# A TensorE loop of nine guarded rounds, a new place for wo among the loads, wider q matmuls and one projection moved ahead, in a decode-attention kernel

## Chip, cores, metric

One core of one Trainium2 chip at a time. The metric is the device time of one execution in microseconds (us); lower is better. A traced execution also has a span, about 1.3 us shorter than its device time.

## The reference, cut to what matters

```python
# x: 1 x 448.  k_cache, v_cache: 8 heads x 65536 x 256, bf16.  16 query heads, two for each KV head.
g = sigmoid((x * gate_w).sum(-1))
a = softmax(((x @ wq) heads) @ k_cache^T / 16) @ v_cache  @ wo     # one query token
b = (relu(x @ W_gate) * (x @ W_up)) @ W_down
out = g * a + (1 - g) * b
```

K and V are 537 MB of the 549 MB that must be read once. One token's arithmetic is small beside that.

## The kernel before

K and V come as 32 + 32 tiles of 8.39 MB (128 partitions of 64 KB). SyncE issues all of these loads, in one order, into three ring slots. A load waits until its slot's last reader is done: the QK matmuls of a K tile, the PV matmuls of a V tile. VectorE transposes K tiles in place (8 instructions a tile) before QK.

The plan gives each operation an engine and a key (a planned time). An engine runs its operations in the order of the keys, so a key decides order alone.

```python
order = [("wq", 0, 8.7), ("k", 0, TILE), ("gu", 0, 7.7), ("wd", 0, 3.8)]
for n in range(1, NT):
    order.append(("k", n, TILE))
    if n >= NTH - 1:
        order.append(("v", n - (NTH - 1), TILE))
for i in range(NT - NTH + 1, NT - 1):          # V 29, V 30
    order.append(("v", i, TILE))
order.append(("wo", 0, 7.3))                   # wo of heads 0 to 4
# then V 31 in five pieces, then the rest of wo in four
...
ROUND = (0, 1, 2, 0, 1, 0, 2, 1)
slot, held, freed = {}, {2: ["gu", "dn"]}, {}  # slot 2 first holds W_gate, W_up, W_down
...
# W_down's projection ("dn"), reading slot 2
l_["dn"] = op("pe", max(tg + 12.2, tL["wd", 0]), f_dn, [l_["hT"], a3])
...
# QK of K tile n, in two halves
qk[n, b] = op("pe", tk + 9 * (b + 1), f_qk(n, b, sl), [tr[4 * b + 3], xcopy, aexp.get(n - 2), c_ps[n % 2]])
...
def emit_loop(self, its, eng, go):             # TensorE: one loop body, seven rounds
    with eng.Fori(0, len(its)):
        for o in its[0]:
            eng.wait_ge(go, 1).then_inc(go, -1)
            o.fn(eng).then_inc(self.esem["pe"], 1)
...
pl.emit("pe", pe[:cut[0]], nc.tensor)          # straight code up to QK of K tile 3
pl.emit_loop(its, nc.tensor, go)               # seven rounds
pl.emit("pe", pe[cut[-1]:], nc.tensor)         # straight code from QK of K tile 31
```

In the loop TensorE doesn't know which semaphore count a round needs; GpSimd waits in its place and gives it one "go" for each operation.

With these keys QK of K tile 0 precedes dn. K tile 2 goes into slot 2, so its load waits for dn.

## Time and profile before

| | before |
|---|---|
| device time, median of 3 | 1278.33 us (1277.96 to 1279.88) |
| the traced execution | 1280.09 us, span 1278.8 us |
| PE, VectorE (DVE) busy | 33%, 50% |
| DMA | 549 MB, 430 GB/s over the span |

The profile's table of slices (40 slices of 32 us; a digit is the busy share in tenths) says what bounds the kernel, and the table of DMA queues tells instruction fetches (q8 is TensorE's) from data:

```profile
PE   3624323334223431224331343321433323233245
...
DVE  2588633465433655434555444555434656335600
...
DMA  9999999999999999999999999999999999999998
...
q1 hardware_dynamic: 12930, 549.03, 99.6%
q8 instruction: 11, 0.18, 0.1%
```

DMA is full everywhere, so time can be gained only where the queue runs dry or works slowly. There is one such place early on. The timeline of before around QK of K tile 0 (start us, length us, engine, line, operation, count, and in brackets the idle time ahead of it with what ended it):

```profile
52.99 6.35 PE L371 MATMUL ST<-ring,xc 128*16 128x512 bf16 x64
...
59.16 1.51 PE L382 MATMUL A_ps<-ring,hT 128*1 128x224 bf16 x28
...
60.70 0.80 SPq L475 DMA_DIRECT2D ring<-in_A_k_cache_dram  x2
...
64.04 17.66 DVE L360 STREAM_TRANSPOSE ring<-ring 128x2048 uint32<-128x2048 uint32 x8 [3.96 <-DMA ring<-in_A_k_cache_dram]
...
84.86 4.50 DVE L360 STREAM_TRANSPOSE ring<-ring 128x2048 uint32<-128x2048 uint32 x2 [3.16 <-DMA ring<-in_A_k_cache_dram]
```

QK of tile 0 (L371), dn (L382), and only then, at 60.70 us, K tile 2's load. The transposes start as soon as a tile has landed: tile 1 at 64.04, tile 2 at 84.86 us, 20.82 us apart, where a tile takes 19.35. The waits of SyncE's queue name the culprit. In the windows of 2 us the last three columns are TensorE's granted clock, the DMA share and GB/s:

```profile
SPq L475 <- PE A_ps L382: 37.9, 1, 37.9
```

```profile
56.00:58.00 2.00, 2.00 (x24) 0.66 (x20) 0.00 (x0) 0.00 (x0) 0.00 (x0) 0.50 1.26 532
58.00:60.00 2.00, 2.00 (x38) 1.23 (x32) 0.61 (x1) 0.00 (x0) 0.00 (x0) 0.90 1.17 496
60.00:62.00 2.00, 0.67 (x14) 0.38 (x10) 0.08 (x1) 1.40 (x2) 0.00 (x0) 1.00 0.96 328
62.00:64.00 2.00, 0.00 (x0) 0.00 (x0) 0.00 (x0) 0.00 (x0) 0.00 (x0) 1.00 0.74 262
```

This view counts a packet with all its time and bytes where it starts, so a single window jumps (before's from 52 to 54 us has a share of 0.53 with 16 packets under way all along). The share of 0.74 from 62 to 64 us therefore doesn't show the hole by itself; the trace's packet records do. Of q1's packets 16 are under way at 60.5 us, 9 at 61.5, 11 at 62, 14 at 63 and 16 again at 64 us. A load is spread over the core's 16 DMA engines, and its semaphore is raised by each of them (16 records for every load of a tile). The trace's semaphore records therefore tell when the first and the last engine finished each load. I call the gap between them the lag.

### The profile page before, as it was taken

How to read it: one execution, taken by the hardware profiler on the slowest of the kernel's cores; microseconds unless marked ns; L12 is line 12 of the kernel's file. 1: busy time of each engine (PE TensorE's matmuls, PEld its weight loads, DVE VectorE, ACT ScalarE, POOL GpSimd, SP SyncE). 2: the span in 40 equal slices, each digit the busy share in tenths (PEclk: the TensorE clock that was granted, in tenths of full speed). 3: DMA queues.
4: the chain of work that ended last, by engine and by line, in shares of the span. 5: the costliest groups of instructions: out<-in, count | busy, mean ns of one | idle time of the engine just before them, and what ended most of it. 6: DMA issues, size and time to landing. Idle time of an engine off the chain costs nothing. (4 is left out here: it accounts for less than half of the span.)

```text
span 1278.8 us, 10158 instructions
## 1 busy us (share of the span) xinstructions
PE 427.7 (33%) x4600; PEld 169.4 (13%) x4600; DVE 633.1 (50%) x421; ACT 63.1 (5%) x124; POOL 4.1 (0%) x21
## 2 busy tenths in 40 slices
PE   3624323334223431224331343321433323233245
PEld 2401101111001110002110111110111101011111
DVE  2588633465433655434555444555434656335600
ACT  0000000000000100001000010000100001000000
POOL 1000000000000000000000000000000000000000
PEclk8555666656666565666656666656666656666567
DMA  9999999999999999999999999999999999999998
GB/s 396 427 427 437 439 429 433 429 445 428 428 433 439 433 433 430 433 441 430 433 433 433 437 433 430 433 435 437 433 433 430 441 433 428 433 435 435 433 413 346
DMA packets 12951, 549.27 MB, mean 430 GB/s; under 512 B 1283, under 2 KB 3590, under 8 KB 3974
## 3 DMA queue, kind: packets, MB, share of 16 engines
q1 hardware_dynamic: 12930, 549.03, 99.6%
q8 instruction: 11, 0.18, 0.1%
q14 instruction: 6, 0.05, 0.0%
q10 hardware_dynamic: 4, 0.00, 0.0%
HBM read 549.03 MB, written 0.00 MB: 429 GB/s over the span
## 5 line engine op out<-in xcount | busy, mean ns | idle before, releaser
L360 DVE STREAM_TRANSPOSE ring<-ring 128x2048 uint32<-128x2048 uint32 x256 | 565.4, 2275 | 399.0 <-DMA ring<-in_A_k_cache_dram 399.0
L371 PE MATMUL ST<-ring,xc 128*16 128x512 bf16 x2048 | 224.9, 614 | 745.8 <-PEq L86 687.6
L371 PEld LDWEIGHTS ST<-ring,xc 128*16 128x16 bf16 x2048 | 66.7, 121 | 889.6 <-issue 827.2
L402 PE MATMUL O<-ring,ptp 128*4 128x512 bf16 x2048 | 150.4, 457 | 34.1 <-DMA ring<-in_A_v_cache_dram 29.8
L486 ACT ACTIVATE P_sb<-ST,nmb 128x512 bf16<-128x512 f32 x32 | 45.1, 1411 | 1103.2 <-DVE nmb L484 1103.2
L484 DVE TENSOR_REDUCE nmb<-ST 128x1 f32<-128x512 f32 x32 | 22.1, 690 | 115.7 <-PE ST L371 115.7
L402 PEld LDWEIGHTS O<-ring,ptp 128*4 128x4 bf16 x2048 | 56.4, 99 | 127.9 <-issue 60.0
L412 DVE CAST o_sb<-O 128x512 bf16<-128x512 f32 x8 | 5.5, 692 | 80.3 <-PE O L402 80.3
L505 DVE TENSOR_TENSOR P_sb<-P_sb,hs 128x1024 bf16<-128x1024 bf16 x16 | 18.9, 1222 | 9.3 <-ACT hs L499 9.3
L510 PE MATMUL PT<-identb,P_sb 128*128 128x128 bf16 x128 | 16.2, 307 | 16.7 <-PEq L86 13.9
L452 PE MATMUL M_ps<-xT,ring 128*128 128x1 bf16 x84 | 9.5, 205 | 16.8 <-DMA ring<-in_B_W_up_dram 16.8
L510 PEld LDWEIGHTS PT<-identb,P_sb 128*128 128x128 bf16 x128 | 12.4, 139 | 19.1 <-issue 16.8
L519 ACT COPY ptp<-PT 128x256 bf16<-128x256 bf16 x32 | 10.3, 375 | 23.8 <-PE PT L510 23.8
L332 PE MATMUL M_ps<-ring,P_sb 128*128 128x256 bf16 x64 | 9.7, 329 | 2.9 <-DMA ring<-in_A_wq_dram 2.9
L452 PEld LDWEIGHTS M_ps<-xT,ring 128*128 128x128 bf16 x84 | 7.2, 152 | 17.4 <-issue 17.0
L486 ACT ACTIVATION_READ_ACCUMULATOR P_sb<-ST,nmb 128x1 f32 x32 | 8.4, 263 | 0.0
L332 PEld LDWEIGHTS M_ps<-ring,P_sb 128*128 128x128 bf16 x64 | 7.5, 119 | 4.9 <-issue 3.0
L455 PE MATMUL M_ps<-xT,ring 128*64 128x1 bf16 x56 | 7.8, 276 | 0.0
L435 DVE STREAM_TRANSPOSE scr<-P_sb 128x128 uint32<-128x128 uint32 x1 | 0.3, 313 | 12.8 <-ACT P_sb L434 12.8
L495 PE MATMUL M_ps<-identf,hs 128*2 128x128 f32 x8 | 2.5, 308 | 10.9 <-PEq L86 9.7
L382 PE MATMUL A_ps<-ring,attnT 128*1 128x224 bf16 x64 | 4.6, 305 | 2.7 <-DMA ring<-in_A_wo_dram 2.7
L455 PEld LDWEIGHTS M_ps<-xT,ring 128*64 128x64 bf16 x56 | 5.4, 191 | 0.4
(74 smaller groups left out, 61.5 us busy)
## 6 DMA issues: line engine op xcount, KB each, us to landing
ring<-in_A_v_cache_dram SPq DMA_DIRECT2D x1, 4096.0 KB, 30.0
ring<-in_A_wq_dram SPq DMA_DIRECT2D x1, 3072.0 KB, 10.2
ring<-in_A_wo_dram SPq DMA_DIRECT2D x1, 2240.0 KB, 32.4
ring<-in_A_v_cache_dram SPq DMA_DIRECT2D x1, 2048.0 KB, 24.6
ring<-in_B_W_down_dram SPq DMA_DIRECT2D x1, 1568.0 KB, 21.2
ring<-in_B_W_gate_dram SPq DMA_DIRECT2D x1, 1344.0 KB, 32.8
ring<-in_B_W_up_dram SPq DMA_DIRECT2D x1, 1344.0 KB, 35.5
ring<-in_A_v_cache_dram SPq DMA_DIRECT2D x1, 1024.0 KB, 26.6
```

The lines of the kernel that those rows point to most:

```text
L332: ins = e.matmul(QN_ps, xw3[:, k_, 31 - j:159 - j], rhs, start=(j == 0 and kt == 0), stop=(j == J - 1 and kt == R3))
L360: return lambda e: e.transpose(v, v)
L371: ins = e.matmul(bank[32 * w:32 * w + 16, :], xc[:, x0:x0 + 16], ktv[sl][:, u0:u0 + 16, c, :, r_], start=(b == 0 and c == 0 and r_ == 0), ...
L402: ins = e.matmul(OP[32 * g:32 * g + 4, :], ptp[:, col:col + 13:4], ring[sl][:, k * 512:(k + 1) * 512], start=(a == 0 and k < 4), stop=(a = ...
L412: o1 = op("dv", tn, lambda e: e.tensor_copy(o_sb[:], OP[:]), [pv[n], last.get(("otr", h - 1))])
L452: e.matmul(GU_ps[:, c:c + 1], wf3[which][:, kt * F + ft:(kt + 1) * F:FT], xT[:, kt:kt + 1], start=(kt == 0), stop=False, skip_group_check= ...
L455: ins = e.matmul(GU_ps[64 * half:64 * half + 64, c:c + 1], wfh[which][:, ft:F // 2:FT], xT[:, R3 + half:R3 + half + 1], start=False, stop= ...
L484: smax[n] = op("dv", tk + 22, lambda e, n=n, NM=NM, t_=t_: e.tensor_reduce(NM[:, t_:t_ + 1], ST[n % 2][:], AX.X, ALU.max, negate=True), [q ...
L486: aexp[n] = op("ac", tk + 23, lambda e, n=n, t_=t_, NM=NM, RS=RS: e.activation(P_sb[:, t_:2048:4], ST[n % 2][:], ACTF.Exp, bias=NM[:, t_:t ...
L505: rsc = op("dv", tt, lambda e, X=X, pb=pb: e.tensor_tensor(pb, pb, X[:, 12:16].unsqueeze(1).to_broadcast([128, 256, 4]), ALU.mult), [h7, a ...
L510: ins = e.transpose(PT[rd][:, s * 128:(s + 1) * 128], P_sb[:, (rd * 8 + s) * 128:(rd * 8 + s + 1) * 128], identb[:, :])
L519: ins = e.copy(dst, src)
```

## The change

The intent: take the first and last heads into TensorE's loop, so that its program is shorter. Rounds 0 and 8 are partial, so each part of the body stands under guards on the round number. Since code in the loop names its ring slot, a tile can be in it only if it has the slot that its place in the round has. V 29 therefore moves to slot 0, which K 31 frees late; wo is loaded ahead of it to fill that time. K 0, V 30 and V 31 don't fit and stay outside. On the side, q is computed with matmuls of 512 columns instead of 256, and dn moves ahead of QK of K tile 0. The diff, cut to its core:

```diff
+        with eng.Fori(0, n) as i:
+            ...
+            for lo, hi, rounds in parts:
+                with ExitStack() as st:
+                    if lo > 0:
+                        st.enter_context(eng.If_ne(i, lo - 1))
+                    if hi < n:
+                        st.enter_context(eng.If_lt(i, hi))
+                    body(rounds[0])
...
-        for i in range(NT - NTH + 1, NT - 1):
-            order.append(("v", i, TILE))
-        order.append(("wo", 0, 7.3))
+        order += [("wo", 0, 7.3), ("v", NT - 3, TILE), ("v", NT - 2, TILE)]
...
+        LASTS = (0, 1, 2, 0, 1, 0)
-                sl = r if m < 0 else ROUND[m % 8] if m < 8 * (H - 1) else m % 8 % 3
+                sl = r if m < 0 else ROUND[m % 8] if m < 8 * (H - 1) else LASTS[m - 8 * (H - 1)]
...
-            for j in range(J):                       # f_q: 16 x 4 matmuls of 256 columns
+            for h in range(H):                       # f_q: 8 x 4 matmuls of 512 columns
...
-                l_["dn"] = op("pe", max(tg + 12.2, tL["wd", 0]), f_dn, [l_["hT"], a3])
+                l_["dn"] = op("pe", tg + 12.2, f_dn, [l_["hT"], a3])
+                assert tg + 12.2 < tL["k", 0] + 20
...
-                    qk[n, b] = op("pe", tk + 9 * (b + 1), f_qk(n, b, sl), [...])
+                    qk[n, b] = op("pe", tk + (9 * (b + 1) if n else 20 + b), f_qk(n, b, sl), [...])
...
+        span = [(1, H + 1), (1, H), (1, H + 1), (0, H), (1, H), (0, H), (1, H)]   # rounds of the seven parts
-        pl.emit("pe", pe[:cut[0]], nc.tensor)
-        pl.emit_loop(its, nc.tensor, go)
-        pl.emit("pe", pe[cut[-1]:], nc.tensor)
+        pl.emit("pe", pe[:heads[0][0]], nc.tensor)
+        pl.emit_loop(H + 1, span, nc.tensor, go)
+        pl.emit("pe", pe[end:], nc.tensor)
```

## The prediction

> **What bounds the kernel now.** The DMA queue. In the table of slices DMA is at 9 in all but the last, while PE is busy 33% and DVE 50% of 1278.8 us. From K tile 3 (landed 104.19 us) to K tile 31 (1187.95 us) the trace's DMA landings are 56 tiles in 1083.76 us: 19.353 us for 8.39 MB, 433.5 GB/s. The Trainium skill, "DMA: Bandwidth & Descriptors", "Where 436 GB/s comes from", gives 435.2 GB/s as ceiling; the trace agrees to 0.4%. All bytes at the measured rate are 1267 us, so only the ends and single stalls can gain.
>
> **What the change does.**
>
> 1. Guards: the loop takes in heads 0 and 7, with more branches on TensorE's sequencer. TensorE waits 22 to 23 us before most QK groups (waits view), and a K tile is issued some 30 us before its own transfer starts (issue to landing 51.3 us), a V tile 17 us. Branches of some us per round are hidden: 0 us.
>
> 2. Fewer instruction fetches. The queue table shows 11 of 16 KB on q8. In the packet records each takes its DMA engine 1.07 us, and the next 64 KB packet there 2.9 instead of 2.42 us: 1.5 us lost on one of 16 engines. The Trainium skill, "Runtime: NRT & Kernel Launch", "Instruction fetch mechanics", says TensorE refills in 16 KiB blocks; the packets agree, and later rounds fetch nothing (none from 245 to 1180 us). I count 2100 instructions of program after, 2800 before: 8 fetches, estimated. It matters only on the engine that finishes last: it lags the first by 2.8 us from tile 2 on, and by 4.34 us after the fetch at 1251 us. Worth 0 to 1.5 us, by luck; I take 0.6.
>
> 3. The hidden part: W_down's projection (dn) now precedes QK of K tile 0. K tile 2's load waits for dn (waits view: 37.9 us, once) and is issued at 60.70 us, only 0.2 us before the first engine runs out of K tile 1. Tiles 1 and 2 land 20.82 us apart instead of 19.35: a hole of 1.47 us, kept to the end. After, dn should run at 53.6 to 55.1 us and the load be issued near 55.2. Gain 1.5 us.
>
> 4. q as 32 matmuls of 512 columns for 64 of 256: the group of 9.67 us shrinks by 1 us (estimated), but W_down and K tile 1 queue behind other loads anyway: 0 us.
>
> 5. wo heads ahead of V 29: same bytes. V 29 waits for K 31's QK (done at 1209.1 us before), and wo's 2.29 MB run out 6 us after V 28. The first engines may idle 1 us, the last, which decides, should not: 0 us.
>
> **Sum.** 1278.3 - 1.5 - 0.6, about 1276.3 us. Range 1274.5 to 1278.3. Faster by over 2%: 1%; within: 98%; slower: 1%.
>
> **What would show it.** K tile 2's load issued near 55 us; K 1 and K 2 landing 19.4 us apart; 19.35 us from tile to tile; 7 to 9 packets on q8; engines at most 4.4 us apart at the last landing; DVE busy unchanged; V 29 issued 2 to 4 us before wo's last packet.
>
> **What would make it wrong.** A fetch that stalls TensorE over 10 us at a skipped part, so that a slot comes free late; refetching in every round (dozens of q8 packets, up to 5 us); fetches on the last engine; V 29 issued after wo's packets end, 1 to 3 us.

## The result and the profile after

| | before | after |
|---|---|---|
| device time, median | 1278.42 us (4 runs, 1277.96 to 1279.88) | 1277.62 us (4 runs, 1277.48 to 1277.77) |
| traced execution, span | 1278.8 us | 1276.2 us |
| TensorE's instruction fetches (q8) | 11 | 8 |
| last landing of the last load (wo) | 1276.59 us | 1273.92 us |

The ratio is 0.9992, interval 0.9974 to 1.0009: the same within 2%, and by this interval not told from no change, though the highest run of after (1277.77) is under the lowest of before (1277.96). Five more rounds below gave 0.9989.

The same views of the kernel after. The slices and the queues first:

```profile
PE   3633322334223431224331343321333313233255
...
DVE  2698633465433655434555444555434655335600
...
DMA  9999999999999999999999999999999999999998
...
q1 hardware_dynamic: 12930, 549.03, 99.7%
q8 instruction: 8, 0.13, 0.0%
```

Then the timeline around QK of K tile 0, where L378 is QK, L389 dn:

```profile
53.73 2.40 PE L389 MATMUL A_ps<-ring,hT 128*1 128x224 bf16 x24 [0.53 <-DVE hT L468]
...
55.92 0.58 PE L389 MATMUL A_ps<-ring,hT 128*1 128x224 bf16 x4
56.13 4.43 PE L378 MATMUL ST<-ring,xc 128*16 128x512 bf16 x62
56.54 4.40 SPq L483 DMA_DIRECT2D ring<-in_A_k_cache_dram  x2
...
63.21 17.66 DVE L367 STREAM_TRANSPOSE ring<-ring 128x2048 uint32<-128x2048 uint32 x8 [1.89 <-DMA ring<-in_A_k_cache_dram]
...
83.50 4.50 DVE L367 STREAM_TRANSPOSE ring<-ring 128x2048 uint32<-128x2048 uint32 x2 [2.63 <-DMA ring<-in_A_k_cache_dram]
```

K tile 2's load is issued at 56.54 us, 5 us before the first engine has finished K tile 1 (61.53 us); in before that margin was 0.75 us (60.70 to 61.45), too little. (The prediction's 0.2 us is the same margin, counted to the end of the first engine's last packet.) SyncE's wait for dn is 3.7 us shorter, and in the packet records 16 packets or more are under way at each half microsecond from 60 to 64 us. The windows:

```profile
SPq L483 <- PE A_ps L389: 34.2, 1, 34.2
```

```profile
60.00:62.00 2.00, 0.56 (x8) 0.06 (x2) 0.69 (x1) 0.65 (x1) 0.00 (x0) 1.00 0.99 426
62.00:64.00 2.00, 0.00 (x0) 0.00 (x0) 0.79 (x1) 0.74 (x2) 0.00 (x0) 1.00 1.14 492
```

Tile 2 still follows tile 1 by 20.29 us at the *last* engine, though the first has its two tiles 19.34 us apart. The difference is lag, and it has to be read engine by engine. The next table is worked out from the DMA semaphore records of the two traces: when the first engine, the mean of the 16 and the last engine had finished a load.

| load landed, us: first / mean / last engine | before | after |
|---|---|---|
| K 1 | 61.45 / 62.21 / 64.02 | 61.53 / 62.05 / 63.18 |
| K 2 | 82.05 / 82.65 / 84.84 | 80.87 / 81.59 / 83.48 |
| K 31 | 1185.14 / 1186.46 / 1187.95 | 1183.86 / 1185.06 / 1186.89 |
| V 28 | 1204.50 / 1205.81 / 1207.30 | 1203.23 / 1204.42 / 1206.25 |
| last wo load | 1272.49 / 1273.93 / 1276.59 | 1272.08 / 1272.77 / 1273.92 |

At K 2 the first engine has gained 1.2 us, and it keeps that through 58 tiles to V 28: nothing is won or lost in between. At the end the last engine has gained 2.67 us, 1.62 us more than at V 28. In before, the fetch at 1251 us fell on the engine that was then last and widened the lag from 2.79 to 4.34 us; in after, none did. But this before-trace is of a run of 1280.09 us, well over its median: a pair of traces isn't the difference of two medians.

### The profile page after: what moved, and what is told of

Its sections match the earlier page's. It is cut to its first block, busy times and chain, and to the rows that moved or that the text cites. A ratio compares the mean times of both kernels' runs of the same rounds, so it can differ in the third digit from the quotient of the medians.

```text
span 1276.2 us, 10216 instructions
## 1 busy us (share of the span) xinstructions
PE 426.9 (33%) x4568; PEld 167.3 (13%) x4568; DVE 633.4 (50%) x421; ACT 63.3 (5%) x124; POOL 4.1 (0%) x21
## 5 line engine op out<-in xcount | busy, mean ns | idle before, releaser
L378 PE MATMUL ST<-ring,xc 128*16 128x512 bf16 x2048 | 223.9, 611 | 745.6 <-PEq L86 745.6
L378 PEld LDWEIGHTS ST<-ring,xc 128*16 128x16 bf16 x2048 | 68.3, 120 | 887.0 <-issue 886.1
L341 PE MATMUL QN<-ring,P_sb 128*128 128x512 bf16 x32 | 8.9, 448 | 3.1 <-DMA ring<-in_A_wq_dram 3.1
L389 PE MATMUL A_ps<-ring,attnT 128*1 128x224 bf16 x64 | 4.6, 306 | 0.7 <-DMA ring<-in_A_wo_dram 0.6
```

The lines of the kernel that those rows point to most:

```text
L341: ins = e.matmul(QN_ps, xw3[:, k_, 31 - h:159 - h], rhs, start=(h == 0 and kt == 0), stop=(h == H - 1 and kt == R3))
L378: ins = e.matmul(bank[32 * w:32 * w + 16, :], xc[:, x0:x0 + 16], ktv[sl][:, u0:u0 + 16, c, :, r_], start=(b == 0 and c == 0 and r_ == 0), ...
```

## Experiments

Medians, ratios to before of the same rounds, and what the trace of one execution each shows. e1 to e4, e5 to e8, e9 and e10, e11 and e12 are four sets on four chips. Where a text below compares medians of different sets, this rests on the kernels with dn early repeating from chip to chip (e2, e8 and e10: 1277.62, 1277.58, 1277.58), while before's medians in the four sets go from 1279.11 to 1279.90. "Hole" is the time between the first engine's landings of K 1 and K 2 less 19.35 us. All gave the correct result.

| run | dn | K 2's load issued | hole | q8 | last landing: first / last engine | device time (5 rounds) | ratio |
|---|---|---|---|---|---|---|---|
| before, traced | late | 60.70 | 1.25 | 11 | 1272.49 / 1276.59 | see above | |
| e1_before_again | late | 59.94 | 0.61 | 11 | 1272.07 / 1275.83 | 1279.68 (1278.97 to 1280.39) | 1.0006 |
| e12_before_third | late | 60.05 | 1.07 | 11 | 1272.10 / 1276.15 | 1279.83 (1279.65 to 1279.98) | 1.0003 |
| e4_dn_undone | late | 59.57 | 0.34 | 8 | 1273.69 / 1275.39 | 1278.59 (1277.78 to 1278.97) | 0.9995 |
| e7_guards_wo | late | 60.30 | 1.33 | 8 | 1274.82 / 1276.55 | 1278.26 (1277.77 to 1280.07) | 0.9989 |
| e11_dn_later | later | 63.57 | 3.87 | 8 | 1275.46 / 1277.18 | 1280.72 (1280.68 to 1281.66) | 1.0012 |
| after, traced | early | 56.54 | 0.0 | 8 | 1272.08 / 1273.92 | see above | 0.9992 |
| e2_after_again | early | 56.45 | 0.0 | 8 | 1272.50 / 1274.40 | 1277.62 (1277.52 to 1277.89) | 0.9989 |
| e3_dn_alone | early | 56.35 | 0.0 | 11 | 1271.48 / 1274.62 | 1277.88 (1277.78 to 1278.12) | 0.9990 |
| e8_q_undone | early | 56.28 | 0.0 | 8 | 1272.74 / 1274.37 | 1277.58 (1277.56 to 1277.87) | 0.9983 |
| e10_wo_undone | early | 56.26 | 0.0 | 8 | 1271.46 / 1274.20 | 1277.58 (1277.54 to 1277.85) | 0.9986 |
| e9_pe_slack | early | 56.29 | 0.0 | 8 | 1272.47 / 1274.31 | 1278.11 (1277.73 to 1278.40) | 0.9990 |
| e5_straight | early | 56.55 | 0.0 | 36 | 1276.44 / 1278.61 | 1282.74 (1282.13 to 1282.84) | 1.0023 |
| e6_wo_between | early | 56.20 | 0.0 | 8 | 1278.70 / 1280.83 | 1283.74 (1283.07 to 1284.33) | 1.0030 |

**e1_before_again**: no edit.

> The unchanged kernel against itself: the noise of the comparison. Theory (the last engine decides, and which engine an instruction fetch hits is luck): the twelve or so times spread over 1 to 2 us, the ratio is 1.000, and the second profile has again a hole of 1.2 to 1.5 us between K tile 1 and K tile 2, but another gap between the first and the last engine at the last landing than the 4.1 us of the first profile. Rival (the gap of 4.1 us belongs to the kernel): again 4.0 to 4.3 us, with the fetch of the tail on the last engine.

Before against itself gave 1.0006 with an interval of 0.0014 to each side: a single ratio here can't show a difference under about 1.5 us. The hole was half as large (0.61 us), so it isn't a constant of the kernel. The final lag was 3.76 us; it came about by 1208 us already (3.97 us), not by a fetch at 1251 us as in the first trace. In that the theory held. In its third trace (e12) it was 4.06 us, which is what the rival expected of the kernel as such. The history of the lag differs from run to run; that it ends near 4 us in all three traces of before I can't call luck any more.

**e2_after_again**: no edit.

> The changed kernel with more rounds. Theory (the hole ahead of K tile 2 is what was gained): 1.0 to 1.5 us under before, ratio 0.9988 to 0.9992, K tiles 1 and 2 landing 19.35 us apart on the first engine, 8 instruction fetches on TensorE's queue. Rival (the difference is noise of the fetches): within 0.4 us of before over five rounds.

Median 1277.62, ratio 0.9989: 1.4 us by the ratio, 1.5 by the medians. Theory held; hole 0.0, 8 fetches.

**e3_dn_alone**: of the whole change, only this, on before:

```diff
-                l_["dn"] = op("pe", max(tg + 12.2, tL["wd", 0]), f_dn, [l_["hT"], a3])
+                l_["dn"] = op("pe", tg + 12.2, f_dn, [l_["hT"], a3])
-                    qk[n, b] = op("pe", tk + 9 * (b + 1), ...
+                    qk[n, b] = op("pe", tk + (9 * (b + 1) if n else 20 + b), ...
```

> Before with one thing changed: dn ahead of QK of K tile 0. Theory: all of the steady gain comes with it, 1.0 to 1.5 us under before, K tile 2's load issued at 55 to 57 us instead of 60.7, 11 fetches as before. Rival (fewer fetches or the order of wo is the gain): within 0.4 us of before, although the load is issued earlier.

1277.88 us, 1.2 us under before's 1279.11 of the same rounds and 0.26 us over e2. Two moved keys brought 1.2 of the change's 1.5 us. The five times lie within 0.34 us, and all are under the lowest of the nine of before (1278.29), so the gain is clear of the noise although the ratio's interval (0.9977 to 1.0004) takes in 1.

**e4_dn_undone**: after, with those two lines put back.

> After with dn put back behind QK of K tile 0. Theory: the hole comes back, K tile 2's load issued near 60 us, the first engine's landings of tiles 1 and 2 20.4 to 20.7 us apart, time back at that of before to 0.4 us. Rival (fewer fetches or the order of wo is the gain): it stays 0.8 us or more under before.

1278.59 us: the hole came back and with it 1.0 us and the spread (1.2 us from lowest to highest). But the size was missed: I expected a hole of 1.0 to 1.3 us and the traced run had 0.34, and the median stayed 0.5 us under before's.

**e5_straight**: after without TensorE's loop: all of its program as straight code, without the relay through GpSimd.

```diff
-        pl.relay(progs, pe[heads[0][0]:end])
-        pl.emit("pe", pe[:heads[0][0]], nc.tensor)
-        pl.emit_loop(H + 1, span, nc.tensor, go)
-        pl.emit("pe", pe[end:], nc.tensor)
+        pl.emit("pe", pe, nc.tensor)
```

> After with no loop for TensorE: the same instructions in the same order, as straight code, waiting on the engines themselves instead of on the relay. Theory: an instruction fetch costs one of the 16 DMA engines 1.5 us, so some 36 fetches instead of 8 cost the mean engine 28 x 1.5 / 16 = 2.6 us: last landing and time 2 to 5 us over after, q8 with 35 to 38 packets, no stall of TensorE. Rival (fetches are hidden: the queue has work ahead): within 0.5 us of after.

1282.74 us, 5.1 us over after, just above the 2 to 5 expected. The queue table of this run, with the fetches:

```profile
q1 hardware_dynamic: 12930, 549.03, 99.4%
q8 instruction: 36, 0.59, 0.2%
```

The rival fell: fetches aren't hidden. TensorE didn't stall for them; it still waited 24 us at the longest for transposes. The DMA engines paid. (The edit also removes the relay through GpSimd. That isn't what cost the time: the first engine landed K 31 at 1183.70 us, as in after, 1183.86, while the last one was already 4.0 us later than in after, 1190.93 against 1186.89.) From K 3 to K 31, with 29 fetches of 16 KB and 3 smaller ones of other engines, the mean engine fell behind the first by 2.96 us more (2.96 x 16 = 47.4 us of engine time; less 3 us for the small ones at about 1 us each, 1.5 us a fetch). That is the price read from single packets in before (1.07 us, plus 2.9 - 2.42 us on the next packet). What the theory had wrong is where they fall. At K 31 the 16 engines were behind the first by

```
0.00 0.15 0.71 0.73 0.74 0.89 1.13 3.29 6.26 6.29 6.35 6.42 6.59 6.62 6.68 7.23   (us)
```

Seven engines had next to nothing of it, one 3.29 us, and eight some 6 to 7 us, four fetches each or so. The last engine thus loses about 1.5 us for every 8 fetches, not for every 16 (its lag grew from 1.97 us at K 3 to 7.23 over 29 fetches).

**e6_wo_between**: after, with wo behind V 29 instead of ahead of it; slots as in after.

```diff
-        order += [("wo", 0, 7.3), ("v", NT - 3, TILE), ("v", NT - 2, TILE)]
+        order += [("v", NT - 3, TILE), ("wo", 0, 7.3), ("v", NT - 2, TILE)]
-        LASTS = (0, 1, 2, 0, 1, 0)
+        LASTS = (0, 1, 0, 2, 1, 0)
```

> After with the first wo heads loaded behind V tile 29 instead of ahead of it; V 29 stays in the ring slot that K tile 31 frees. Theory: V 29 can be issued only at about 1208 us, when K 31's QK is done, and the queue has run dry at 1203 (first engine) to 1206 us (last): a hole of 3 to 5 us, time 2.5 to 4.5 us over after. Rival (the place of wo among the loads does not matter, the bytes are the same): within 0.5 us of after.

1283.74 us, 6.1 us over after, more than the 2.5 to 4.5 expected. The first line of its timeline merges the issues of V 28 (at 1174.48 us) and V 29, which ends 34.70 us later, after K 31's QK; the windows show a queue with nothing to do meanwhile:

```profile
1174.48 34.70 SPq L550 DMA_DIRECT2D ring<-in_A_v_cache_dram  x2
1209.22 0.43 SPq L563 DMA_DIRECT2D ring<-in_A_wo_dram  x1
```

```profile
1200.00:1204.00 4.00, 0.00 (x0) 0.00 (x0) 4.00 (x3) 0.00 (x0) 0.00 (x0) 0.81 0.68 295
1204.00:1208.00 4.00, 2.78 (x28) 1.05 (x32) 1.02 (x1) 0.00 (x0) 0.00 (x0) 0.50 0.00 0
1208.00:1212.00 4.00, 1.43 (x11) 0.37 (x3) 1.47 (x5) 1.85 (x4) 0.00 (x0) 0.84 0.74 262
```

At the last engine V 28 and V 29 landed 24.14 us apart (1206.67 and 1230.81): 4.8 us of hole. The rest came with the fetch at 1241 us, which this time hit one of 16 engines that the hole had put level: the lag went from 0.70 to 2.24 us. So the order of the loads does matter once V 29 has to wait for K 31's slot.

**e7_guards_wo**: after with dn and q put back: guards and wo order alone.

> After with dn and q both put back: the guarded loop and the order of wo alone. Theory: neither is worth over 0.5 us but for luck with fetches; K tile 2's hole is back; time 0 to 0.8 us under before (9 fetches instead of 11, mean engine 0.2 us). Rival (the guards cost TensorE time that reaches the loads): K tile issues later than in before and more than 0.5 us over before.

Median 1278.26, but 1277.77 to 1280.07 in five runs: inconclusive as a time, and the 1.6 us by the medians under before's 1279.90 (1.4 by the ratio) are more than I expected. The trace has the hole (1.33 us). What it does settle is the rival: the best of its runs are as fast as after, so guards cost nothing that shows.

**e8_q_undone**: after with q in 64 matmuls of 256 columns.

> After with q back to 64 matmuls of 256 columns. Theory: W_down and K tile 1 are issued 0.5 us later (near 21.9 us instead of 21.5), behind loads that keep the queue busy, so 0: within 0.4 us of after, K tile 2 issued near 56.5 us. Rival (the shorter q is the gain): back at before.

1277.58 against 1277.62 us: the shorter q is worth nothing.

**e9_pe_slack**: after with 24 idle matmuls ahead of each V tile's PV (0 to 29), into a PSUM bank that nothing reads.

```diff
             def f_pv(e):
+                if n < NT - 2:
+                    for _ in range(24):
+                        e.matmul(QN_ps, identb[:, :], ring[sl][:, 0:512], start=True, stop=True)
```

> After with 24 idle matmuls of 512 columns (into a PSUM bank that nothing reads) ahead of the PV of V tiles 0 to 29: 6 to 10 us more TensorE time before each such slot comes free, far more than branches can cost. Theory (loads are issued 17 to 30 us before their turn, so the guards cost nothing): tiles still land 19.35 us apart, time within 0.8 us of after (one more instruction fetch, and PV 29's idle matmuls come before the pieces of V 31 are issued, which still have V 30 ahead of them). Rival (TensorE's time in the loop reaches the loads): spacing over 19.4 us, time many us over.

PE's busy time rose by 162 us in all, 5.4 us for each of 30 tiles; the first line of this run's page and its group of idle matmuls:

```profile
PE 589.4 (46%) x5288; PEld 233.1 (18%) x5288; DVE 633.4 (50%) x421; ACT 62.9 (5%) x124; POOL 4.1 (0%) x21
```

```profile
L408 PE MATMUL QN<-ring,identb x720: 379/379/634, 131.9 to 1239.1; 128*128 128x512 bf16 x180
```

The time rose by 0.5 us; from K 2 to K 31 the first engine needed 1103.02 us against 1102.99 in after. So in the middle of the kernel some 5 us of TensorE time before each V tile's slot comes free are hidden, and a few branches with them. (5.4 us a tile is less than the 6 to 10 I had expected.)

**e10_wo_undone**: after with wo behind V 30 and V 29 in its old slot, so V 29's PV outside the loop.

> After with the first wo heads loaded behind V tile 30 again, V 29 back in the slot that K tile 30 frees (so its PV leaves the loop). Theory: V 29 is issued at about 1174 us and no engine idles at 1209 us; the mean engine gains 0.2 to 0.3 us against after, the last engine nothing, and TensorE fetches one more block of 16 KB: within 0.5 us of after. Rival (the order of wo is a gain in itself): 1 us or more over after.

1277.58 us: the same as after. The mean engine's last landing was 1272.62 us against 1272.77, the last engine's 1274.20 against 1273.92. The new order of wo makes the shorter loop possible without a loss; it isn't a gain. (e9 and e10 were each expected to fetch one block more than after, and e7 nine blocks; all three have 8 on q8.)

**e11_dn_later**: e4 with 12 idle matmuls of 512 columns ahead of dn, to make the hole larger by a known size.

> After with dn behind QK of K tile 0 (as in the fourth run) and 12 idle matmuls of 512 columns ahead of it: the suspected wait made longer by a known size, 2.6 to 3 us at the full clock. Theory (the hole ahead of K tile 2 goes straight to the end): K tile 2 issued at 62.3 to 63.5 us, a hole of 3 to 4.3 us between tiles 1 and 2 on the first engine, time 2.3 to 3.5 us over the fourth run's 1278.6, so 1281 to 1282. Rival (the hole is made good later or hidden): under 1279.5.

The timeline of this run (the trace has 11 of the 12; some records are missing):

```profile
53.11 6.30 PE L378 MATMUL ST<-ring,xc 128*16 128x512 bf16 x64
59.56 2.54 PE L475 MATMUL QN<-ring,identb 128*128 128x512 bf16 x11 [0.16 <-issue]
62.03 1.51 PE L389 MATMUL A_ps<-ring,hT 128*1 128x224 bf16 x28
...
63.57 1.51 SPq L484 DMA_DIRECT2D ring<-in_A_k_cache_dram  x2
```

Hole 3.87 us, time 1280.72 us: 2.1 us over e4 (which ran on another chip; 2.2 by the ratios to before) and 3.1 over after. The rival (under 1279.5) fell; the size was just under what I expected (2.3 to 3.5 over e4). That a hole of 3.9 us costs only 3.1 would fit lagging engines that still work while the first ones idle: the lag at V 28 is 2.16 us here, 3.02 in after and 3.28 in e2. This isn't shown by a run of its own.

**e12_before_third**: no edit; for the question why the hole varies.

> Before a third time, to test a relation found in four profiles with dn late: the earlier TensorE's clock goes from 0.5 to 1.0 during QK of K tile 0, the shorter QK, the earlier dn, and the earlier K tile 2's load (granted clock from 56 to 58 us of 0.50, 0.57, 0.78, 0.96 went with an issue at 60.70, 60.30, 59.94, 59.57 us). Theory: the new pair lies on that line to 0.2 us, and times again spread over 1 us or more, while kernels with dn early stay within 0.5 us. Rival (no relation): off the line.

The windows from 56 to 58 us of e4 and then of e12 (the third number from the right is TensorE's granted clock; before's own, 0.50, stands above):

```profile
56.00:58.00 2.00, 2.00 (x36) 0.89 (x30) 0.00 (x0) 0.00 (x0) 0.00 (x0) 0.96 1.13 492
```

```profile
56.00:58.00 2.00, 2.00 (x32) 0.78 (x28) 0.00 (x0) 0.00 (x0) 0.00 (x0) 0.76 1.26 532
```

| dn late | granted clock, 56 to 58 us | QK of K 0 took | K 2's load issued |
|---|---|---|---|
| before | 0.50 | 6.35 us | 60.70 us |
| e7 | 0.57 | 6.15 us | 60.30 us |
| e12 | 0.76 | 5.67 us | 60.05 us |
| e1 | 0.78 | 5.69 us | 59.94 us |
| e4 | 0.96 | 5.44 us | 59.57 us |

The fifth trace lies on the line of the first four to 0.1 us. The clock doubles while QK of K 0 runs, sooner in one run and later in another; with QK ahead of dn, that moves K 2's load by 1.1 us, just where the queue is about to run dry. With dn early it can't. What differs from run to run can be read too: in each of the fourteen traces every stretch of one granted clock but the last is a whole multiple of 3.413 us long (in before 6.83 us at 1.0 from 17.44 us on, 34.13 at 0.5, 6.83 at 1.0), and this grid lies differently against each kernel's start, so that the doubling came at 56.17 us in e4 and at 58.40 in before. That this is how the times spread is made likely by the series, not shown run by run, since untraced runs have no such record: before ranged from 1277.96 to 1280.80 us over all its rounds, and the four kernels with dn early that make no extra work or holes (after with e2, e3, e8, e10; 24 runs) lie between 1277.48 and 1278.12, where only one of before's 50 timed runs (e1 and e12 among them) lies. The 1.1 us that the traces show are less than half of before's range of 2.8 us, so something else must spread it too. The five timed runs of e12 itself lay within 0.33 us, against what I had expected, although the nine of before beside them spread over 1.8.

## Why the prediction was right, and where its sizes were off

1. **The bound.** Right. From K 2 to V 28 nothing changed: the first engine took 1122.4 us in both traces (82.05 to 1204.50, 80.87 to 1203.23). The 433.5 GB/s of the prediction stayed.
2. **Guards: 0 us.** Right; e9 hides 5.4 us a tile. The room was overstated, though: of the 62 waits ahead of QK groups in before's trace 21 are over 20 us, and the 31 ahead of a tile's second half are 5.2 to 5.6 us.
3. **Fetches: 8 for 11, "I take 0.6".** The count was right, the size about twice what it measured: e3 (11 fetches) is 0.26 us over e2 (8), less than the spread of five runs of either (0.34 and 0.37 us), and the two differ in the guards, q and wo as well. A fetch's price of 1.5 us of one engine held in e5. That each fetch is "lost on one of 16 engines" held; that they spread over all 16, as e5's expectation counted on, was wrong: they fall on eight. The Trainium skill, "Runtime: NRT & Kernel Launch", "Instruction fetch mechanics", calls crossing a 16 KiB boundary "mostly hidden". For TensorE that agrees with e5; for a kernel bound by DMA it doesn't: 28 more fetches went with 5.1 us (the last load landed 4.2 us later than in e2).
4. **dn ahead of QK: 1.5 us.** The mechanism was right (e3, e4, e11). The term was mis-sized: alone it measured 1.2 us in e3. I took 1.47 us from the last engine of one trace (its first engine has 1.25), and that one was of a slow execution (1280.09 us against a median of 1278.33) in which the clock had doubled late; other traces of before have holes of 0.61 and 1.07 us. dn itself also ran at half clock, 2.8 us instead of the 1.5 forecast, so the load came at 56.54 us and not at 55.2; with 5 us in hand that cost nothing.
5. **q: 0 us.** Right (e8).
6. **wo ahead of V 29: 0 us.** Right (e10). As forecast, the first engines idled: V 29 was issued at 1208.11 us, 4.0 us before wo's last engine was done (1212.10), and the lag shrank from 3.02 us at V 28 to 2.12 at V 29, the last engine not being held. e6 shows the cost when wo isn't there to fill this time.

The sum said 2.1 us; measured were 0.8 us in the first comparison and 1.4 to 1.5 in e2. The forecast of 1276.3 us was 1.3 us low, inside its range: term 4 by 0.3, term 3 by 0.3, and the rest because the median of 1278.33 us that I subtracted from was of three runs of a kernel whose median came out at 1278.42 to 1279.90 in later sets. What stays open is why the final lag of the engines is near 4 us in all three traces of before and about 3 in e3 and e10, which end with loads in the same order, and why e4 and e7, with dn late, stayed 0.5 and 1.6 us under before, more than e3 leaves for the rest of the change. No experiment beat after by more than the noise.

## What to carry to other kernels

Where the DMA queue is the limit, look for the load that is issued last before the queue runs dry, and ask what stands ahead of it in program order on the engine that frees its buffer: here, two moved keys alone (e3) brought 1.2 of the 1.5 us that the whole change brought with its rebuilt loop, merged matmuls and new load order. Read landings at the first, mean and last DMA engine, not only at the semaphore's last count: here the holes showed at the first, the instruction fetches at the last. And before taking a size from one trace, compare that execution's time with the median; if it is off, the trace shows the mechanism, not the typical size.

## What the Trainium skill lacked or had wrong

- "Runtime: NRT & Kernel Launch", "Instruction fetch mechanics": it has TensorE's fetches of 16 KiB blocks (the packets agree) but not their cost to data traffic: 1.5 us of one DMA engine each, and TensorE's fall on 8 of the 16 engines (e5: seven engines with a lag of at most 1.13 us, eight with 6.26 to 7.23). 36 fetches instead of 8 went with 5.1 us more.
  It also warns that a taken branch out of the fetched window stalls the engine. Here a loop body of about 1100 instructions (my count) with skipped parts ran nine rounds with no fetch from 108 to 1241 us; fetches at 66 and 72 us, which before, e3 and e5 without guards don't have, came with the parts skipped in round 0 and delayed no load; whether TensorE stalled for them was not read.
- "TensorE: Matmul & The Clock Gate", "Part 1: The HAM clock gate", gives about 3.4 us of sustained work until the full clock. Here TensorE showed busy 2.00 of every 2.00 us from 40 to 56 us, with matmuls of one column up to 53 us, at a granted clock of 0.50; it doubled only 3.4 to 5.4 us into QK with 512 columns (six traces with dn late). So a busy share of 1 in this profile was not enough for the full clock. That the moment varies from run to run, as the page says, agrees: 0.50 to 0.96 in the same window of five traces.
